# A new order of all operations up to the third set of the feed-forward, with ssm_k loaded in quarters ahead of v

## The chip, the core and the metric

The kernel runs on one core of a Trainium2 chip. Five engines work from queues of their own, each in the order of its queue: TensorE (PE, with its weight loads PEld), VectorE (DVE), ScalarE (ACT), GpSimd (POOL) and SyncE (SP), which issues all DMAs here. An instruction waits on semaphores of other engines, and everything behind it on its engine waits with it. The metric is the device time of one execution in microseconds. Before: 643.6 us, the median of 3 runs (643.42 to 643.73).

## The reference

```python
def _A_ref(q, k, v, shift_k, ssm_k, ssm_D):
    ...                                    # k_shift: causal depthwise conv of k, 4 taps
    kv = k_shift * v
    L = 2 * S
    ...                                    # y: irfft(rfft(kv) * rfft(ssm_k)) over S = 2048, per channel
    y = y + kv * ssm_D[None, None, :]
    return q * y
def _B_ref(x, w_gate, w_up, w_down):
    g = _silu(x @ w_gate)
    u = x @ w_up
    return (g * u) @ w_down
x = A_q
mod = (_silu(c) @ w_mod).reshape(c.shape[0], 6, 1, -1)
sa, ca, ga, sb, cb, gb = (mod[:, 0], mod[:, 1], mod[:, 2], mod[:, 3], mod[:, 4], mod[:, 5])
h = _layernorm(x, axis=-1) * (1 + ca) + sa
x = x + ga * _A_ref(h, A_k, A_v, A_shift_k, A_ssm_k, A_ssm_D)
h = _layernorm(x, axis=-1) * (1 + cb) + sb
x = x + gb * _B_ref(h, B_w_gate, B_w_up, B_w_down)
```

One sequence of 2048 tokens, 512 channels, 1792 hidden columns, all float32.

## The kernel before

**The convolution.** The 512 channels go in four blocks of 128 (index `c_` or `b`, 0 to 3). For a block, DVE (or ACT for the first tap) makes the four taps `u` from `kt` (`tap0`, `tap`), multiplies by `vt` (`times_v`), PE turns the product (`x_turn`, tile `kvt`, copied by ACT to `x`) and takes the first step of a transform (`x_first`, tile `s`, copied by ACT into `X`). The filter goes the same way: `k_first` (tile `s` from `ss`, the loaded ssm_k; ACT copies into `kt`) and `k_turn` (tile `kt`, copied into `K`). `load_e` loads the transform's matrix `er` in quarters, and `skip` adds ssm_D to one row of `ss` on DVE, which is why the quarter of `k_first` that holds this row waits for DVE.

**Sixteen pieces.** `X` and `K` of a block hold four pieces of 32 channels. For piece n, `swap_x` transposes 32 by 32 blocks of `X` in place (DVE), `x2nd` takes the second step (PE tile `px`, ACT copies it to `xs`), `product` takes it for `K` twice (PE tile `pk`) and multiplies with `xs` (two DVE operations `R`), and `inv` goes back (PE tile `iv`, ACT copies into the piece of `X`). A second `swap_x` by block follows on the blocks that are not stored; blocks 0, 1 and 2 are stored to memory instead (`put`, tile `away`) and read back in swapped order (`get`, `X<-away`), and block 3 is swapped by DVE. `y_pe` makes the outputs `y` of token set t (four sets of 512 tokens) and some blocks, `y_gate` multiplies them into `S1[t]` (tile `s`), and `add_c` or `add_y` adds that to `x`.

**The gate of layer norm.** `do_stats` (DVE, with four small operations on POOL that end in `rsa`), then `do_gate`: four ACT operations `s<-x,rsa` of 512 columns and two POOL operations `s<-s,bcs` of 2048 columns for one token set. `mod_load`, `mod_part`, `mod_bc`, `mod_T` and `mod_mix` make the six modulation vectors (tiles `wm`, `pb`, `part`, `pm`, `modT`, `bcs`).

**The feed-forward.** It takes 14 sets of 128 hidden columns for each half of the tokens. Sets 0 and 1 of the first half are written out one by one (`gu_pe`, `gu_act`, `gu_end`, tiles `g`, `sg`, `acts`), between the normalisations of token sets 0 and 1 (`norm2a`, `norm2b`: tile `n`; `norm_t`: tile `nt`; `norm_s`: tile `hraw`) and the splits into high and low parts (`op_hi`, `op_lo`, `w8_hi`, `w8_lo`, `wd_hi`, `wd_lo`). From the third set on (n = 2 to 27), `gate_up` computes two token sets with seven products (`seventh`, tiles `a`, `b`, `c`, `d`, six matmuls each) with four `down`s (tile `dn`, six matmuls each) between them; `split_w` prepares the next set's weights on ACT and POOL (`wa`, `sr`, `wsum`). The table `AT` hangs other work behind a product of a set; `half_t` is there the normalisation's turn for token sets 2 and 3 (two `nt` tiles, copied by ACT to `hraw`).

**What sets the order.** All engines are wrapped so that the program's order is kept: each engine executes its instructions in the order in which the code calls the helpers. Before, a loop over the 16 pieces (`loop`) with a table of hooks sets the order of the front: at each n `product(n)`, `x2nd(n + 1)`, `swap_x(n + 2)`, hooks, `inv(n - 1)`, hooks. The four PSUM buffers `ps` of two banks, the tags `e8` (8 buffers), `b16` (6), `r4` (5) and `f16` (1) are handed out as they come free.

In the profile nearly all instructions carry L40, the wrapper's line, so steps are told by their tiles.

Of the kernel before, what the change touches and what calls it, by code (L numbers as in the profile page):

```python
# [10 lines left out]
F32 = mybir.dt.float32  # L11
# [5 lines left out]
P = 128  # L17
# [26 lines left out]
def adaln_h3_swiglu(ctx, tc, q, kT, vT, shk, ssm, dskip, wgu, wdn, c, wmod, e_fwd, e_inv, w_c, out):  # L44
# [28 lines left out]
    def bank(name):  # L73
        return banks(name)[:, 0]
# [210 lines left out]
    def loop(hooks):  # L285
        for n in range(PIECES + 1):
            if n < PIECES:
                product(n)
            if n + 1 < PIECES:
                x2nd(n + 1)  # L290
            if n + 2 < PIECES:
                swap_x(n + 2)
            for f in hooks.get(n, ()):
                f()
            if n > 0:
                inv(n - 1)
            for f in hooks.get((n,), ()):
                f()

# [13 lines left out]
    def mod_part(i):  # L313

        ps = bank(f"pb{i}")
        for t in range(4):
            pe.matmul(ps[32 * t : 32 * t + 32], csb[:, t, :], WM[i][:, t, :], start=True, stop=True)
        part[i] = k2([P, D], F32, f"part{i}")
        act.copy(part[i], ps)
# [62 lines left out]
    def normal(dst, t, rs, both=True):  # L382

        for i in range(4):
# [9 lines left out]
    def gate(t):  # L394
# [328 lines left out]
    def load_ssm(c_):  # L723
        SS[c_] = e8([P, J, P], F32, f"ss{c_}")
        sp.dma_start(SS[c_], ssm[:, c_])
# [5 lines left out]
    load_k(0)  # L731
    load_e(0)
    load_e(1)
    load_ssm(0)
    load_e(2)
    load_e(3)
    load_v(0)
    load_k(1)
    load_v(1)
    wc = cp.tile([P, 4, 64], F32, name="wc")  # L740
    sp.dma_start(wc, w_c)
    W2, W2S, V1, V2 = (wc[:, i, :] for i in range(4))
    def kf(c_, *jqs):
        return [lambda jq=jq: k_first(c_, jq) for jq in jqs]

    def kt(c_, *ms):
        return [lambda m=m: k_turn(c_, m) for m in ms]

    def run(fs):
        for f in fs:  # L750
            f()

    tap0(0, dve)
    tap(0, 1)
    load_ssm(1)
    skip(0)
    run(kf(0, 0, 1, 2, 3))
    tap(0, 2)
    tap(0, 3)
    times_v(0, dve)  # L760
    x_turn(0, 0)
    x_turn(0, 1)
    x_first(0, 0)
    run(kt(0, 0, 1))
    x_first(0, 1)
    run(kt(0, 2, 3))
    tap0(1, dve)
    for t in range(1, KS):
        tap(1, t)
    load_k(2)  # L770
    swap_x(0)
    swap_x(1)
    x2nd(0)
    times_v(1, dve)
    load_v(2)
    tap0(2, act)
    skip(1)
# [5 lines left out]
    def do_stats(t):  # L783
        st1.append(stats(xt[t], f"a{t}"))

    def do_gate(t):
        if t < 2:
            S1[t] = e8([P, 4, D], F32, f"s{t}")
        else:
            if t == 2:  # L790
                S1["b"] = b16("s23", (P, 8, D))
            S1[t] = S1["b"][:, 4 * (t - 2) : 4 * (t - 1), :]
        gate(t)

    def add_c(t, *cs):
# [271 lines left out]
```

## Time and profile before

| what | value |
|---|---|
| median of 3 runs | 643.6 us |
| the profiled execution, its own time | 643.63 us |
| its span, first to last instruction | 641.9 us |
| PE busy | 601.9 us (94%) |
| DVE busy | 472.3 us (74%) |
| ACT, POOL busy | 299.5 us, 315.5 us |
| mean granted TensorE clock | 0.984 |
| first product of the third set (`a`) starts at | 232.29 us |

The profiled execution lies 1.73 us above its span, and at the median of the runs. Up to 232.29 us lies the front that the change reorders; behind it 26 sets of the feed-forward run at one speed. A busy share of PE is not a share of useful time where the granted clock is below 1.

### The profile page before, as it was taken

How to read it: one execution, taken by the hardware profiler on the slowest of the kernel's cores; microseconds unless marked ns; L12 is line 12 of the kernel's file. 1: busy time of each engine (PE TensorE's matmuls, PEld its weight loads, DVE VectorE, ACT ScalarE, POOL GpSimd, SP SyncE). 2: the span in 40 equal slices, each digit the busy share in tenths (PEclk: the TensorE clock that was granted, in tenths of full speed). 3: DMA queues.
4: the chain of work that ended last, by engine and by line, in shares of the span. 5: the costliest groups of instructions: out<-in, count | busy, mean ns of one | idle time of the engine just before them, and what ended most of it. 6: DMA issues, size and time to landing. Idle time of an engine off the chain costs nothing.

```text
span 641.9 us, 9081 instructions
## 1 busy us (share of the span) xinstructions
PE 601.9 (94%) x3604; PEld 454.8 (71%) x3604; DVE 472.3 (74%) x600; ACT 299.5 (47%) x439; POOL 315.5 (49%) x248
## 2 busy tenths in 40 slices
PE   2899999989697899999999999999999999999997
PEld 2756456534276788777778888878888888888885
DVE  5998767957978688877766886898565665656655
ACT  1867667874124545454544443544343333333320
POOL 0000000599254479775673767486565757575400
PEclk9999999989889999999999999999999999999999
DMA  8884492953931121302022111114210112120003
GB/s 293 370 300 161 165 234 86 269 103 137 242 115 66 34 67 33 99 33 67 20 79 66 34 34 65 34 66 154 75 67 34 65 38 86 43 65 1 0 2 131
DMA packets 30107, 64.68 MB, mean 101 GB/s; under 512 B 2289, under 2 KB 14705, under 8 KB 27506
## 3 DMA queue, kind: packets, MB, share of 16 engines
q1 hardware_dynamic: 30066, 64.11, 31.7%
q8 instruction: 28, 0.46, 0.3%
q14 instruction: 13, 0.11, 0.1%
HBM read 53.62 MB, written 10.49 MB: 100 GB/s over the span
## 4 chain that ended last, share of the span: by engine, by line
PE 54%; DVE 16%; ACT 5%; issue 2%; POOL 1%; ACTq 0%; DVEq 0%; POOLq 0%
PE dn L40 19%; PE b L40 9%; PE a L40 8%; PE c L40 8%; PE d L40 5%; DVE d L40 2%; DVE x L40 2%; PE y L40 2%; DVE acts L40 2%; DVE n L40 1%; DVE X L40 1%; ACT acts L40 1%; ACT op L40 1%; PE pk L40 1%; DVE c L40 1%
## 5 line engine op out<-in xcount | busy, mean ns | idle before, releaser
L40 PE MATMUL dn<-wd,acts 128*128 128x512 f32 x672 | 165.9, 390 | 0.5 <-DVE acts L40 0.5
L40 PEld LDWEIGHTS dn<-wd,acts 128*128 128x128 f32 x672 | 126.0, 188 | 27.9 <-DVE acts L40 1.1
L40 POOL TENSOR_TENSOR wa<-ws,wa 128x512 fp32r<-128x512 f32 (+1 forms) x52 | 60.6, 1188 | 110.9 <-ACT wa L40 103.1
L40 DVE TENSOR_TENSOR x<-x,dn 128x512 f32<-128x512 f32 x112 | 74.6, 680 | 54.4 <-PE dn L40 53.3
L40 PE MATMUL b<-op,wsum 128*128 128x512 f32 x312 | 79.7, 391 | 0.8 <-POOL wsum L40 0.8
L40 POOL TENSOR_TENSOR wsum<-sr,wsum 128x1024 fp32r<-128x1024 f32 x26 | 72.3, 2779 | 0.0
L40 PEld LDWEIGHTS b<-op,wsum 128*128 128x128 f32 x312 | 58.1, 188 | 13.3 <-POOL wsum L40 1.3
L40 POOL TENSOR_SCALAR rsa<-mva 128x4 f32<-128x4 f32 x8 | 2.5, 310 | 118.5 <-DVE mva L40 118.0
L40 PE MATMUL a<-op,wa 128*128 128x512 f32 x228 | 57.9, 389 | 0.0
L40 ACT ACTIVATE sg<-sg 128x512 f32<-128x512 f32 x26 | 16.5, 633 | 87.4 <-DVE sg L40 87.4
L40 DVE TENSOR_TENSOR R<-pk,xs 128x1024 f32<-128x1024 f32 x32 | 37.7, 1215 | 25.2 <-PE pk L40 25.2
L40 PEld LDWEIGHTS a<-op,wa 128*128 128x128 f32 x228 | 42.8, 188 | 8.9
L40 DVE STREAM_TRANSPOSE X<-X 128x1024 f32<-128x1024 f32 x20 | 45.3, 2277 | 0.1
L40 POOL TENSOR_TENSOR wd<-wds,wd 128x1024 fp32r<-128x1024 f32 x14 | 35.5, 2538 | 19.6 <-ACT wd L40 19.6
L40 ACT CAST acts<-d 128x512 fp32r<-128x512 f32 x26 | 15.3, 587 | 62.9 <-DVE d L40 36.5
L40 POOL TENSOR_TENSOR sr<-ws 128x256 f32<-128x256 f32 x52 | 43.1, 828 | 0.0
L40 PE MATMUL c<-op,wa 128*128 128x512 f32 x156 | 39.7, 390 | 0.0
L40 PE MATMUL d<-op,wsum 128*128 128x512 f32 x156 | 39.6, 389 | 0.0
L40 PE MATMUL c<-op,wsum 128*128 128x512 f32 x156 | 39.6, 389 | 0.0
L40 POOL TENSOR_TENSOR s<-s,bcs 128x2048 f32<-128x2048 f32 x8 | 36.5, 4568 | 0.3
L40 PE MATMUL pk<-K,wc 64*64 64x512 f32 x256 | 35.3, 626 | 1.1 <-ACT K L40 1.0
L40 DVE TENSOR_TENSOR op<-hraw,op 128x1024 fp32r<-128x1024 f32 x14 | 23.1, 1654 | 15.2 <-ACT op L40 15.2
(105 smaller groups left out, 1095.9 us busy)
## 6 DMA issues: line engine op xcount, KB each, us to landing
ws<-in_wgu SPq DMA_DIRECT2D x28, 512.0 KB, 3.3
wds<-in_wdn SPq DMA_DIRECT2D x14, 512.0 KB, 3.6
wm<-in_wmod SPq DMA_DIRECT2D x6, 1024.0 KB, 11.4
away<-X SPq DMA_DIRECT2D x3, 2048.0 KB, 7.5
X<-away SPq DMA_DIRECT2D x12, 512.0 KB, 11.2
kt<-in_kT SPq DMA_DIRECT2D x4, 1024.0 KB, 5.4
ss<-in_ssm SPq DMA_DIRECT2D x4, 1024.0 KB, 10.0
vt<-in_vT SPq DMA_DIRECT2D x4, 1024.0 KB, 10.1
```

What stands on the lines that cost most here:

```text
L40: return lambda *a, **k: self.tc.keep_in_program_order(f(*a, **k))
```

## The change

The hooks and the loop go. The calls from the first load to the end of set 1 now stand in one list of 324 calls, which sets the order on all engines; the operations are the same, with these differences: `load_ssm(0)` loads four quarters, two of them ahead of the matrix and all ahead of `v`; `times_v` is called by quarters, the stats and the four ACT operations of a gate by halves, the gate's POOL part by itself (`gate_p`); four `warm(6)` (six small matmuls that nothing reads) in place of one `warm(4)`; and `half_t` hangs one product later in its sets. `kx_first` and `swap_k` are new and called nowhere.

```diff
+    def gate_n(t, half):
+
+        if half == 0:
...
+        normal(lambda i: S1[t][:, i, :], t, st1[t], False, range(2 * half, 2 * half + 2))
+
+    def gate_p(t):
         s = S1[t]
-        normal(lambda i: s[:, i, :], t, st1[t], False)
         pool.tensor_tensor(s, s, bcs[:, None, 1, :].to_broadcast([P, 4, D]), op=ALU.mult)
         pool.tensor_tensor(s, s, bcs[:, None, 0, :].to_broadcast([P, 4, D]), op=ALU.add)
...
-    def load_ssm(c_):
-        SS[c_] = e8([P, J, P], F32, f"ss{c_}")
-        sp.dma_start(SS[c_], ssm[:, c_])
+    def load_ssm(c_, *jqs):
+        if c_ not in SS:
+            SS[c_] = e8([P, J, P], F32, f"ss{c_}")
+        for jq in jqs:
+            sp.dma_start(SS[c_][:, 4 * jq : 4 * jq + 4], ssm[:, c_, 4 * jq : 4 * jq + 4])
+        if not jqs:
+            sp.dma_start(SS[c_], ssm[:, c_])
...
+    warm(6)
+    warm(6)
+    load_k(0)
+    tap0(0, dve)
+    tap(0, 1)
+    load_ssm(0, 0)
+    load_ssm(0, 2)
+    load_e(2)
+    k_first(0, 2)
...
-        (5, 2): lambda: half_t(2, 0),
+        (5, 3): lambda: half_t(2, 0),
         (6, 7): lambda: norm2b(2, rs[2], 1),
-        (6, 2): lambda: half_t(2, 1),
-        (6, 3): lambda: norm_stats(3, range(0, 2)),
+        (6, 3): lambda: half_t(2, 1),
+        (6, 2): lambda: norm_stats(3, range(0, 2)),
...
-        (7, 2): lambda: half_t(3, 0),
+        (7, 3): lambda: half_t(3, 0),
         (8, 7): lambda: norm2b(3, rs[3], 1),
-        (8, 2): lambda: half_t(3, 1),
+        (8, 3): lambda: half_t(3, 1),
```

**The start, on SP.** The rows are the first large DMAs, before: `kt`, `vt` are k and v of a block, `ss` its filter, `er` the matrix in quarters.

```order
L40 DMA kt_93<-in_kT 128x2048
L40 DMA er<-in_e_fwd 128x512 x2
L40 DMA ss_97<-in_ssm 128x2048
L40 DMA er<-in_e_fwd 128x512 x2
L40 DMA vt_101<-in_vT 128x2048
L40 DMA kt_103<-in_kT 128x2048
L40 DMA vt_105<-in_vT 128x2048
L40 DMA wc<-in_w_c 128x256
L40 DMA ss_112<-in_ssm 128x2048
```

The same place in the changed kernel:

```order
L40 DMA kt_108<-in_kT 128x2048
L40 DMA ss_113<-in_ssm 128x512 x2
L40 DMA er<-in_e_fwd 128x512 x4
L40 DMA ss_113<-in_ssm 128x512 x2
L40 DMA vt_191<-in_vT 128x2048
L40 DMA wc<-in_w_c 128x256
L40 DMA kt_230<-in_kT 128x2048
L40 DMA ss_242<-in_ssm 128x2048
L40 DMA vt_293<-in_vT 128x2048
```

Two quarters of the first filter now stand ahead of the matrix, and the second block's filter ahead of its v.

**The gates, on ACT.** Before, around the gates of token sets 1, 2 and 3 (`s<-x,rsa`); `K_1255` is K of block 3, `X_642` X of block 2, `kt_1147` the filter of block 3 before its turn:

```order
L40 COPY xs<-px 128x1024
L40 ACTIVATE s_1140<-x_920,rsa_1058 128x512 x4
L40 COPY kt_1147<-s_1148 128x4x4x32 x2
L40 COPY kt_1147<-s_1159 128x4x4x32 x2
L40 COPY X_642<-iv 128x32x32
L40 COPY kt_1147<-s_1180 128x4x4x32 x2
L40 COPY kt_1147<-s_1191 128x4x4x32 x2
L40 COPY xs<-px 128x1024
L40 ACTIVATE s_1248<-x_922,rsa_1135 128x512 x4
L40 COPY K_1255<-kt 128x1024 x2
L40 COPY X_642<-iv 128x32x32
L40 COPY K_1255<-kt 128x1024 x2
```

In the changed kernel, around the gates of sets 1, 2 and 3 (`K_1221` is K of block 3, `X_747` X of block 2):

```order
L40 ACTIVATE s_1153<-x_834,rsa_1090 128x512 x4
L40 COPY X_747<-iv 128x32x32
L40 COPY xs<-px 128x1024 x2
L40 COPY X_747<-iv 128x32x32
L40 COPY K_1221<-kt 128x1024 x3
L40 COPY X_747<-iv 128x32x32 x2
L40 COPY K_1221<-kt 128x1024
L40 COPY xs<-px 128x1024
L40 ACTIVATE s_1306<-x_868,rsa_1166 128x512 x2
L40 ACTIVATE s_1306<-x_980,rsa_1322 128x512 x4
L40 ACTIVATE s_1306<-x_868,rsa_1166 128x512 x2
L40 COPY xs<-px 128x1024
```

The copies of K of block 3 moved ahead of the gates of token sets 2 and 3, which now stand together ahead of the copy to `xs` of piece 13.

**The last outputs, on PE.** Before, the end of the pieces and the first outputs of block 2 (`X_642`) and block 3 (`X_987`); `pb` are two modulation vectors:

```order
L40 MATMUL iv<-R,wc 64x512 x8
L40 MATMUL pk<-K_1255,wc 64x512 x8
L40 MATMUL iv<-R,wc 64x512 x16
L40 MATMUL y<-X_642,ei 64x128 x8
L40 MATMUL y<-X_987,ei 64x128 x8
L40 MATMUL pb_1535<-wm,csb 32x512 x4
L40 MATMUL pb_1542<-wm,csb 32x512 x4
```

In the changed kernel (`X_267` and `X_470` are X of blocks 0 and 1, `X_884` of block 3, `X_747` of block 2):

```order
L40 MATMUL iv<-R,wc 64x512 x16
L40 MATMUL y<-X_267,ei 64x128 x8
L40 MATMUL y<-X_470,ei 64x128 x8
L40 MATMUL pb_1545<-wm,csb 32x512 x4
L40 MATMUL y<-X_884,ei 64x128 x8
L40 MATMUL y<-X_747,ei 64x128 x8
L40 MATMUL warm<-ident 128x128 x6
L40 MATMUL pb_1587<-wm,csb 32x512 x4
```

An output of blocks 0 and 1 (token set 3) and one vector now stand between the last `iv` and the first output of block 3, and that one stands ahead of the one of block 2. On SP, `mod_load(3, 4)` moved from behind `get(2)` to ahead of it.

More of the change, by code (lines that the diff above doesn't have):

```diff
@@ L729, in skip, with load_wc @@
         dve.tensor_tensor(t, t, dsk[:, c_ * P : (c_ + 1) * P], op=ALU.add)
[L731 to L739, printed above, removed]
     wc = cp.tile([P, 4, 64], F32, name="wc")
-    sp.dma_start(wc, w_c)
     W2, W2S, V1, V2 = (wc[:, i, :] for i in range(4))
[L743 to L777, printed above, removed]
+    def load_wc():
+        sp.dma_start(wc, w_c)
     def mod_mix():
@@ new lines, in adaln_h3_swiglu @@
+    tap(0, 2)
+    tap(0, 3)
+    load_e(1)
+    load_ssm(0, 1)
+    k_first(0, 1)
+    load_ssm(0, 3)
+    k_first(0, 3)
+    k_turn(0, 0)
+    k_turn(0, 1)
+    load_v(0)
+    times_v(0, 3)
+    times_v(0, 2)
+    times_v(0, 1)
+    load_wc()
+    x_turn(0, 1)
+    k_turn(0, 3)
+    times_v(0, 0)
+    x_turn(0, 0)
+    load_k(1)
+    k_turn(0, 2)
+    load_ssm(1)
+    k_first(1, 2)
+    k_first(1, 1)
+    x_first(0, 0)
+    tap0(1, dve)
+    tap(1, 1)
+    tap(1, 2)
+    tap(1, 3)
+    load_v(1)
@@ new lines, in adaln_h3_swiglu @@
+    times_v(1, 3)
+    times_v(1, 0)
+    x_first(0, 1)
+    mod_load(1, 2)
+    mod_part(1)
+    k_first(1, 3)
+    skip(1)
+    times_v(1, 2)
+    times_v(1, 1)
+    k_first(1, 0)
+    mod_part(2)
+    x_turn(1, 1)
+    k_turn(1, 0)
+    load_k(2)
+    k_turn(1, 3)
+    swap_x(1)
+    swap_x(2)
+    tap0(2, act)
+    mod_bc(2)
+    x_turn(1, 0)
+    load_v(2)
+    swap_x(0)
+    k_turn(1, 1)
+    swap_x(3)
+    load_ssm(2)
+    skip(2)
+    k_turn(1, 2)
+    mod_bc(1)
+    tap(2, 1)
+    x2nd(0)
@@ new lines, in adaln_h3_swiglu @@
+    tap(2, 2)
+    tap(2, 3)
+    times_v(2, 2)
+    times_v(2, 3)
+    k_first(2, 3)
+    mod_load(0, 5)
+    times_v(2, 0)
+    x_first(1, 0)
+    x_first(1, 1)
+    mod_part(5)
+    k_first(2, 0)
+    load_ssm(3)
+    product(0)
+    x2nd(1)
+    x2nd(2)
+    swap_x(5)
+    load_k(3)
+    product(1)
+    tap0(3, act)
+    tap(3, 1)
+    skip(3)
+    times_v(2, 1)
+    k_first(2, 1)
+    inv(0)
+    k_first(2, 2)
+    inv(1)
+    tap(3, 2)
+    mod_part(0)
+    tap(3, 3)
+    k_turn(2, 0)
+    k_turn(2, 2)
@@ new lines, in adaln_h3_swiglu @@
+    k_turn(2, 1)
+    load_v(3)
+    product(2)
+    x2nd(3)
+    times_v(3, 0)
+    product(3)
+    x_turn(2, 0)
+    inv(2)
+    inv(3)
+    mod_bc(0)
+    times_v(3, 3)
+    x_turn(2, 1)
+    x_first(2, 0)
+    times_v(3, 1)
+    x_turn(3, 0)
+    times_v(3, 2)
+    load_x(0)
+    swap_x(4)
+    do_stats(0, 0)
+    k_turn(2, 3)
+    swap_x(6)
+    do_stats(0, 1)
+    x2nd(4)
+    product(4)
+    load_x(1)
+    x_turn(3, 1)
+    swap_x(7)
+    x_first(2, 1)
+    load_x(2)
+    swap_x(10)
+    swap_x(9)
@@ new lines, in adaln_h3_swiglu @@
+    k_first(3, 2)
+    x_first(3, 0)
+    do_stats(2, 0)
+    x2nd(5)
+    x_first(3, 1)
+    k_first(3, 3)
+    product(5)
+    swap_x(8)
+    x2nd(6)
+    swap_x(13)
+    x2nd(7)
+    load_x(3)
+    inv(4)
+    inv(5)
+    product(6)
+    put(0)
+    product(7)
+    mod_bc(5)
+    get(0)
+    mod_mix()
+    gate_n(0, 0)
+    inv(6)
+    inv(7)
+    put(1)
+    k_first(3, 1)
+    do_stats(1, 0)
+    do_stats(1, 1)
+    x2nd(8)
+    x2nd(9)
+    swap_x(11)
+    k_first(3, 0)
+    product(8)
+    product(9)
@@ new lines, in adaln_h3_swiglu @@
+    gate_n(0, 1)
+    gate_p(0)
+    gate_n(1, 0)
+    gate_n(1, 1)
+    gate_p(1)
+    do_stats(2, 1)
+    inv(8)
+    x2nd(10)
+    swap_x(14)
+    product(10)
+    x2nd(11)
+    swap_x(12)
+    inv(9)
+    k_turn(3, 0)
+    k_turn(3, 1)
+    k_turn(3, 3)
+    product(11)
+    load_einv()
+    swap_x(15)
+    inv(10)
+    inv(11)
+    k_turn(3, 2)
+    x2nd(12)
+    gate_n(2, 0)
+    do_stats(3, 0)
+    do_stats(3, 1)
+    gate_n(3, 0)
+    product(12)
+    gate_n(3, 1)
+    get(1)
+    gate_n(2, 1)
@@ new lines, in adaln_h3_swiglu @@
+    y_pe(0, 0, 1)
+    y_gate(0, 0, 1)
+    add_c(0, 0)
+    y_pe(1, 0, 1)
+    y_gate(1, 0, 1)
+    x2nd(13)
+    gate_p(3)
+    add_c(1, 0)
+    put(2)
+    inv(12)
+    x2nd(14)
+    product(13)
+    product(14)
+    swap_x(12)
+    inv(13)
+    mod_load(3, 4)
+    get(2)
+    swap_x(13)
+    warm(6)
+    x2nd(15)
+    product(15)
+    inv(14)
+    inv(15)
+    y_pe(3, 0, 1)
+    mod_part(3)
+    swap_x(14)
+    swap_x(15)
+    y_pe(0, 3)
+    gate_p(2)
+    add_c(0, 1)
+    y_pe(0, 2)
+    warm(6)
```

277 lines of the change are left out of this document (126 added, 151 removed).

## The prediction

> **What bounds the kernel now.** I read the timeline of PE first, to find where the feed-forward's steady run begins, then the busy times by stretch ahead of that point.
>
> ```profile
> 232.29 1.52 PE L40 MATMUL a<-op,wa 128*128 128x512 f32 x6
> ```
>
> This is the first product of the third set. Behind it PE runs nearly without a gap, and the only edit there is the place of `half_t`. So the question is when this row starts.
>
> ```profile
> core 0: us, PE busy (x) PEld busy (x) DVE busy (x) ACT busy (x) POOL busy (x), PEclk, DMA share, GB/s
> 0.00:12.31 12.31, 0.00 (x1) 0.01 (x1) 5.06 (x11) 1.49 (x2) 0.69 (x6) 1.00 0.74 249
> 12.31:42.00 29.69, 26.91 (x284) 21.43 (x288) 29.46 (x22) 21.47 (x25) 0.00 (x0) 1.00 0.84 334
> 42.00:112.00 70.00, 69.00 (x683) 37.34 (x676) 54.16 (x46) 48.28 (x60) 0.00 (x0) 1.00 0.61 182
> 136.00:152.00 16.00, 12.55 (x77) 4.41 (x75) 8.26 (x10) 10.75 (x14) 15.60 (x8) 0.79 0.01 5
> 152.00:182.00 30.00, 24.11 (x232) 11.75 (x234) 27.14 (x43) 7.51 (x10) 13.34 (x6) 0.83 0.96 264
> 182.00:204.00 22.00, 21.33 (x223) 18.90 (x220) 14.95 (x30) 8.72 (x11) 10.88 (x9) 1.00 0.13 48
> 204.00:216.00 12.00, 7.85 (x35) 6.16 (x33) 8.24 (x8) 8.36 (x11) 3.96 (x4) 0.86 0.15 46
> 216.00:232.29 16.29, 15.78 (x70) 13.06 (x70) 12.32 (x10) 6.11 (x9) 13.45 (x9) 1.00 0.11 33
> ```
>
> First number the length, then busy time by engine, granted clock, DMA. DVE fills 12 to 42 us (29.46 of 29.69), PE fills 42 to 112 (69.0 of 70). Behind 136 neither is full, and the clock falls below 1 in three stretches.
>
> **PE's work up to 232.29.** A step costs PE the distance to the next start where PE never waits:
>
> ```profile
> 45.61 1.95 PE L40 MATMUL pk<-K,wc 64*64 64x512 f32 x16
> 47.38 1.04 PE L40 MATMUL px<-X,wc 64*64 64x512 f32 x8
> 48.34 2.06 PE L40 MATMUL s<-er,ss 64*128 64x128 f32 x32
> 50.36 1.95 PE L40 MATMUL iv<-R,wc 64*64 64x512 f32 x16
> 52.23 2.06 PE L40 MATMUL s<-er,ss 64*128 64x128 f32 x32
> ...
> 100.24 2.06 PE L40 MATMUL kt<-ident,kt 128*128 128x128 f32 x16
> 102.14 1.88 PE L40 MATMUL pb<-part,sel 128*128 128x512 f32 x4
> 103.96 1.95 PE L40 MATMUL pk<-K,wc 64*64 64x512 f32 x16
> ...
> 152.23 1.97 PE L40 MATMUL y<-X,ei 128*64 128x128 f32 x32 [0.59 <-ACT X L40]
> 154.12 1.95 PE L40 MATMUL iv<-R,wc 64*64 64x512 f32 x16
> ...
> 233.65 1.52 PE L40 MATMUL b<-op,wsum 128*128 128x512 f32 x6
> 235.01 1.52 PE L40 MATMUL c<-op,wsum 128*128 128x512 f32 x6
> ```
>
> So `product` 1.77, `x2nd` 0.96, two `k_first` 2.02, `inv` 1.87, two turns about 2.0, a vector about 0.95, a `y` of two blocks 1.89, six large matmuls 1.36. Sixteen of each piece step: 28.3 + 15.4 + 30.0. `k_first` 16.5, `x_first` 15.9 (of the same shape), 24 turns 24.0, `y` 15.1, vectors 9.5 and their turns 1.9, `nt` 3.9, 96 `g` 21.8, 24 `dn` 5.4, `warm` 1.0: **188.8 us**. The row starts at 232.3, so PE loses **43.5 us** ahead of it.
>
> ```profile
> 7.67 1.28 DVE L40 TENSOR_SCALAR u<-kt,shk_sb 128x2048 f32<-128x2048 f32 x1 [3.16 <-DMA kt<-in_kT]
> 12.31 6.17 PE L40 MATMUL s<-er,ss 64*128 64x128 f32 x64 [12.31 <-DVE ss L40]
> 16.93 2.50 DVE L40 TENSOR_TENSOR vt<-u,vt 128x512 f32<-128x512 f32 x4
> 112.75 1.95 PE L40 MATMUL pk<-K,wc 64*64 64x512 f32 x16
> ...
> L40 DVE STREAM_TRANSPOSE X<-X 128x1024 f32<-128x1024 f32 x20 | 45.3, 2277 | 0.1
> L40 DVE SCALAR_TENSOR_TENSOR u<-kt,shk_sb,u 128x2047 f32<-128x2047 f32 (+2 forms) x12 | 28.0, 2329 | 0.3
> ```
>
> Where: 12.3 us ahead of the first matmul, 2.8 idle in 12 to 42, and 2.1 because the first 64 `s` take 6.17 us where the warm ones take 4.04: 17.2. The `pk` row at 112.75 is that of piece 9; ahead of it stand 94.5 us of the work above, so the loss is 18.2 by then: only 1 us more over 70, the running loss of a full PE, about 2%. The other 25 lie behind: 136 to 152 3.5 idle plus 0.21 of the clock, 6.8 together; 152 to 182 5.9 + 5.1 = 11.0; 204 to 216 4.2 + 1.7 = 5.8; little elsewhere.
>
> **The change: the start.** DVE has the path. It must do, ahead of the first `R`: two blocks with 1.28 + 3 x 2.33 + 2.50 each, 21.5; four swaps, 9.1; three taps and three quarters of `times_v` for block 2, 8.9; three skip adds, together about 0.8 by estimate: 40.3. From 7.67 that is 48.0. PE's list up to and with `product(0)` then ends at about 48.5, with 37.7 us of useful work done: a loss of **10.8** where it was 17.2. Loading the filter in quarters lets the first `k_first` run while DVE makes taps; that fills PE, not the path, and costs SP three more issues, hidden while data, not issues, fill the queue. If `v` came later by them, DVE would wait as long: k, filter, matrix and v are 4.19 MB, and v is wanted at 16.0.
>
> ```profile
> GB/s 293 370 300 161 165 234 86 269 103 137 242 115 66 34 67 33 99 33 67 20 79 66 34 34 65 34 66 154 75 67 34 65 38 86 43 65 1 0 2 131
> ```
>
> The first slice of 16 us moves 293 x 16.05 = 4.70 MB, so it is there. The two first `warm` stand in the wait and cost nothing.
>
> **The middle.** From `product(0)` to the outputs I added PE's and DVE's operations in the new order call by call: they stay within 3 us of each other, with steps of other pieces between each `product` and its `inv`. I take the same 2% of running loss, on 150 us: 3.0 (bounds 1 and 6). Splitting stats, gates and `times_v` changes no sum; the work that hides a split's later half is the other engine's queue.
>
> **The late part.**
>
> ```profile
> 134.64 9.17 POOL L40 TENSOR_TENSOR s<-s,bcs 128x2048 f32<-128x2048 f32 x2
> 134.72 2.93 ACT L40 ACTIVATE s<-x,rsa 128x512 f32<-128x512 f32 x4 [2.08 <-POOL rsa L40]
> 138.60 1.16 PE L40 MATMUL kt<-ident,kt 128*128 128x128 f32 x8 [2.13 <-ACT K L40]
> ...
> 152.20 0.34 SPq L40 DMA_DIRECT2D away<-X  x1
> 172.87 1.97 PE L40 MATMUL y<-X,ei 128*64 128x128 f32 x16 [3.93 <-DMA X<-away]
> ```
>
> (a) 136 to 152. Before, ACT waits for POOL's small `rsa` behind 9.2 us of gate work, and the copies of K that PE needs stand behind it. In the new order those copies stand ahead. What is late next is the copy to `xs` of piece 13, behind four pairs of ACT operations for sets 2 and 3 (twice the 2.93 of the row, 5.9 us) and behind `rsa` of set 2, which now has two gates ahead on POOL, 18.3 us. By my sum gate 0 starts near 114, `rsa` comes at 134, the copy at 141; PE has two `y`, two `x2nd` and an `inv` until then. I take 2 of the 6.8 (bounds 0 and 7).
>
> (b) 152 to 182. Block 2's way out and back took 172.87 - 152.20 = 20.7 us with the pieces nearly done. In the new order 28 us of PE work stand between `inv(11)` and the first `y` that reads it, so 3.9 us of wait and the slow clock behind it go; `wm` stands ahead of it on SP and takes some of the margin. Left is DVE: from `R` of piece 13 to the last swap three products at 2.4 and four swaps, 16.3 us, against 15.3 on PE, and a wait for the last two. I take 3.5 of 11.0 (bounds 2 and 8).
>
> (c) 204 to 216. Before, PE had only `n` of token set 1 to turn and waited for it; now products of sets 0 and 1 stand between. I take 2 of 5.8 (bounds 0 and 5).
>
> Sum of the loss: 10.8 + 3.0 + 2 + 3.5 + 2 = 21.3. PE's work: 188.8 - 1.0 + two `warm(6)` of about 1.4 = 190.6. The row comes at **211.9**, 20.4 earlier.
>
> The trace has the clock at 0.79 in 136 to 152 behind a gap of only 2.13 us in a stretch of thin work.
>
> [...]
>
> **The change: half_t.**
>
> ```profile
> 296.57 0.27 PE L40 MATMUL nt<-ident,n 128*128 128x128 f32 x1
> 298.05 0.98 PE L40 MATMUL nt<-ident,n 128*128 128x128 f32 x7 [1.22 <-DVE n L40]
> ...
> L40 PE MATMUL nt<-ident,n 128*128 128x128 f32 x32 | 5.0, 280 | 4.0 <-DVE n L40 4.0
> ```
>
> Four turns wait for `n`, 4.0 us together. One product later (1.36 us) the wait of 1.22 is covered; ACT's and DVE's orders do not change, and PE alone ends last there. I take **4.0** (bounds 3 and 4).
>
> **The sum.** 643.6 - 20.4 - 4.0 = **619.2**, from the profiled execution's 643.63 (span 641.9 and 1.7 around it), which is the runs' median. With all low bounds (loss 13.8) 612, with all high ones (36.8 less what cannot add, since a late `xs` also covers the swaps: about 28) 626.
>
> **Rivals.** *The wait moves to the first outputs.*
>
> ```profile
> 110.84 0.33 SPq L40 DMA_DIRECT2D away<-X  x1
> 119.26 7.11 SPq L40 DMA_DIRECT2D X<-away  x4
> 136.00:138.00 2.00, 0.47 (x5) 0.27 (x3) 1.61 (x5) 2.00 (x4) 2.00 (x1) 1.00 0.07 29
> ```
>
> Block 1 leaves at 110.84 and the queues are empty only from 136: 25 us, with the outputs' matrix among it. In the new order `y` of token set 0 stands ahead of four `inv`, with 27 us of PE work since block 1's last `inv`. The margin is 2 us. If it fails by 6, or if gate 0 starts as late as before and `rsa` comes 9 later, PE loses that and some 4 at the slow clock: **631** (626 to 638). For: the margin; against: block 2's trip took only 20.7.
>
> *Slower.* The clock. In 42 to 112 PE is full and the clock stays 1.00; at 136 to 138 PE is busy for 0.47 of 2 us, and slow matmuls follow. If the tight coupling of PE and DVE leaves PE short gaps everywhere, it runs slow from 20 to 200 us, and each 10 us at half clock costs 5 of progress. It outweighs the 24.4 from 50 slow microseconds on; at 70 it gives **654**. Against: the sums keep both engines full, and gaps of 1.2 us before cost no clock.
>
> [...]
>
> *The order brings nothing*, one engine's queue giving back elsewhere what it gains: 643.6.
>
> **Chances.** Forecast (612 to 626) 0.64; late outputs 0.20; better than 612 0.06; nothing 0.03; slower 0.07. The range 611 to 634 leaves out 0.05 below and some 0.15 above. About 0.2% can be told from no change: faster 0.90, same 0.03, slower 0.07.
>
> **What would show it.** `a` of the third set near 212. The first `R` near 48. `K` copies ahead of `s<-x,rsa`, and no PE gap of 2 us at the `kt` of block 3. No wait for `X<-away` at `y`. The wait of `nt` for `n` gone. It would be wrong if `y` of token set 0 waits for a DMA, if ACT waits for `rsa` past 140, or if the clock falls below 0.9 over more than 20 us.

## The result, and the profile after

The changed kernel took **620.37 us** (median of 4 runs, 619.95 to 620.67), the kernel before beside it 643.54 (643.42 to 643.73): a ratio of 0.9639, with a 95% interval of 0.9623 to 0.9656. Forecast were 619.2, in 611 to 634. The profiled execution is the run of 619.95, with a span of 618.2 us; its clock is 0.990 where it was 0.984.

The place that the prediction turned on, on PE's timeline of the changed kernel:

```profile
213.92 1.52 PE L40 MATMUL a<-op,wa 128*128 128x512 f32 x6
```

The third set starts 18.4 us earlier (232.29 before); forecast was 211.9, 20.4 earlier. Behind it the loop takes 618.2 - 213.92 = 404.3 us, where it took 641.9 - 232.29 = 409.6: 5.3 less, forecast 4.0. Together 23.7 of span. The busy times by stretch of the changed kernel, up to that row (length, then busy time by engine, the granted clock, the DMA share and GB/s):

```profile
0.00:8.60 8.60, 4.94 (x24) 4.75 (x24) 2.36 (x8) 1.49 (x2) 0.69 (x6) 1.00 0.66 215
8.60:48.00 39.40, 37.06 (x420) 31.66 (x420) 38.33 (x28) 32.68 (x45) 0.00 (x0) 0.91 0.99 385
48.00:112.00 64.00, 64.00 (x652) 33.85 (x654) 58.90 (x59) 45.74 (x57) 3.35 (x8) 1.00 0.58 177
112.00:136.00 24.00, 23.75 (x234) 12.25 (x228) 22.48 (x26) 16.84 (x20) 21.70 (x12) 1.00 0.98 227
136.00:152.00 16.00, 14.77 (x142) 6.11 (x142) 15.86 (x18) 8.05 (x10) 13.94 (x3) 1.00 1.12 248
152.00:182.00 30.00, 26.68 (x302) 19.74 (x295) 28.00 (x54) 11.59 (x14) 11.32 (x9) 1.00 0.36 101
182.00:212.00 30.00, 25.25 (x112) 20.77 (x111) 27.27 (x19) 13.94 (x21) 28.49 (x17) 0.94 0.16 53
```

Read the column of PE against the length: from 48 to 136 almost nothing is lost, and the clock is 1.00 to 182, also in 136 to 182, where it was 0.79 and 0.83. What is left stands at the two ends: the start, and the last 30 us, where POOL (28.49 of 30) and DVE (27.27) are nearly full and PE is not. That last stretch is the miss: 4.75 idle and 6% of clock on 30, 6.5 us, where 2 were forecast.

What PE waits for up to 214, longest group first, by the view of waits of the changed kernel (us in total, times, longest):

```profile
PE nt L40 <- DVE n L40: 4.4, 2, 3.0
PE s L40 <- DMA er<-in_e_fwd: 3.5, 1, 3.5
PE iv L40 <- DVE R L40: 1.8, 2, 1.2
PE dn L40 <- POOL wd L40: 1.7, 1, 1.7
```

No `y` waits for a block that comes back from memory. And in the chain of the changed kernel PE has 83% where it had 54%:

```profile
PE 83%; DVE 8%; ACT 3%; issue 2%; POOL 2%; DMA 1%; SPq 0%; ACTq 0%; DVEq 0%; POOLq 0%
```

### The profile page after: what moved, and what is told of

It reads as the page before. It is cut to its first block, busy times and chain, and to the rows that moved or that the text cites. A ratio compares the mean times of both kernels' runs of the same rounds, so it can differ in the third digit from the quotient of the medians.

```text
span 618.2 us, 9164 instructions
## 1 busy us (share of the span) xinstructions
PE 598.0 (97%) x3644; PEld 460.1 (74%) x3644; DVE 482.6 (78%) x601; ACT 298.7 (48%) x439; POOL 319.6 (52%) x248
## 4 chain that ended last, share of the span: by engine, by line
PE 83%; DVE 8%; ACT 3%; issue 2%; POOL 2%; DMA 1%; SPq 0%; ACTq 0%; DVEq 0%; POOLq 0%
PE dn L40 24%; PE a L40 11%; PE b L40 11%; PE c L40 11%; PE d L40 6%; PE s L40 5%; PE iv L40 3%; PE pk L40 3%; PE kt L40 3%; DVE R L40 2%; PE px L40 2%; DVE n L40 1%; PE pb L40 1%; PE kvt L40 1%; DVE x L40 1%
## 5 line engine op out<-in xcount | busy, mean ns | idle before, releaser
L40 POOL TENSOR_TENSOR wa<-ws,wa 128x512 fp32r<-128x512 f32 (+1 forms) x52 | 62.1, 1216 | 108.4 <-ACT wa L40 100.5
L40 PEld LDWEIGHTS b<-op,wsum 128*128 128x128 f32 x312 | 58.6, 188 | 12.2
L40 ACT ACTIVATE sg<-sg 128x512 f32<-128x512 f32 x26 | 16.5, 633 | 87.6 <-DVE sg L40 87.6
L40 DVE TENSOR_TENSOR acts<-c,acts 128x512 fp32r<-128x512 f32 x26 | 18.0, 691 | 21.8 <-ACT acts L40 21.8
L40 PEld LDWEIGHTS c<-op,wa 128*128 128x128 f32 x156 | 29.2, 188 | 6.3 <-DVE op L40 0.2
## 6 DMA issues: line engine op xcount, KB each, us to landing
wm<-in_wmod SPq DMA_DIRECT2D x6, 1024.0 KB, 12.4
```

The lines of the kernel that those rows point to most:

```text
L40: return lambda *a, **k: self.tc.keep_in_program_order(f(*a, **k))
```

## The experiments

Each kernel is the changed one with one edit, but for the sixth, which is the one before. All were timed in five rounds beside the kernel before. Two distances compare their traces better than absolute times: from the first `R` to the first `a` of the third set, and from there to the end of the span. The first `R` itself lies anywhere between 48.7 and 50.3 in the kernels whose start is that of the change.

| kernel | us, median | ratio to before, 95% | first `R` | `R` to `a` | `a` to end |
|---|---|---|---|---|---|
| as changed | 620.37 | 0.9623 to 0.9656 | 49.36 | 164.6 | 404.3 |
| 1 loads as before | 622.5 | 0.9660 to 0.9687 | 51.10 | 165.8 | 403.7 |
| 2 half_t back | 624.84 | 0.9705 to 0.9734 | 48.85 | 164.9 | 409.0 |
| 3 gates ahead of K | 632.77 | 0.9817 to 0.9852 | 49.45 | 176.3 | 404.3 |
| 4 no warm | 623.33 | 0.9669 to 0.9696 | 49.22 | 166.2 | 404.3 |
| 5 warm through | 622.34 | 0.9655 to 0.9697 | 48.40 | 168.2 | 403.9 |
| 7 n on ACT | 620.59 | 0.9632 to 0.9665 | 50.32 | 166.6 | 404.0 |
| 8 wd first | 621.63 | 0.9644 to 0.9670 | 50.18 | 164.9 | 405.3 |
| 9 adds late | 620.54 | 0.9625 to 0.9651 | 49.16 | 160.9 | 408.6 |
| 10 gate behind n | 622.75 | 0.9663 to 0.9689 | 49.60 | 167.0 | 404.3 |
| 11 warm late | 624.47 | 0.9685 to 0.9714 | 48.72 | 168.0 | 404.3 |
| 12 both of 7 and 8 | 619.96 | 0.9623 to 0.9649 | 48.93 | 164.9 | 404.0 |

**1. The loads of the start.**

```diff
+    load_e(0)
+    load_e(1)
+    load_ssm(0)
+    load_e(2)
+    load_e(3)
+    load_v(0)
...
-    load_ssm(0, 0)
-    load_ssm(0, 2)
-    load_e(2)
...
-    load_ssm(0, 3)
...
-    load_v(0)
```

> The changed kernel (620.4 us) with the loads of the start in the order of before: k, two quarters of the matrix, the first filter in one piece, the other two quarters, v. Theory: the new order of loads fills PE with the first k_first, but DVE has the path to the first R, so it is worth little: 620.5 to 622, first R within 1 us of 49.4. Rival: the loads bring the gain of the start (some 5 us): 624 to 627, first R at 53 or later.

It took 622.5, 2.1 more, with the first `R` at 51.10, 1.7 later: a little above the theory's range and well below the rival's. The timeline of DVE in this kernel shows by which way:

```profile
11.84 0.28 DVE L40 TENSOR_TENSOR ss<-ss,bcs 1x128 f32<-1x128 f32 x1 [1.08 <-DMA ss<-in_ssm]
31.98 2.31 DVE L40 STREAM_TRANSPOSE X<-X 128x1024 f32<-128x1024 f32 x1 [1.61 <-ACT X L40]
```

The skip add is one of DVE's operations and needs the filter, so with the whole filter in one transfer DVE itself waits 1.08; then its swaps wait 1.61 for X, which PE and ACT make, where they wait 0.56 in the changed kernel (at 30.26). The quarters are on DVE's path, not only on PE's. What the profiled execution loses beyond these 1.7 us is lost far behind the loads: from the first `dn` to `a` it takes 7.2 us where the changed kernel takes 5.6, partly at a clock of 0.50, behind a wait of 2.55 for `wd` (the last section has what the traces show of the clock behind a wait).

**5. More warm matmuls at the start.**

```diff
     warm(6)
     warm(6)
+    warm(6)
+    warm(6)
     load_k(0)
```

> The changed kernel with four warm(6) at the start in place of two, so that PE stays busy from 1.35 to about 9.5, when the first data come. Theory: the clock then stays at 1.00, but the first 64 s follow the arrival of the matrix and the filter, not the clock (without any warm they took 5.51 from 10.60 and ended at 16.1, where with two they took 6.70 from 9.77 and ended at 16.5), so the first R moves by less than 0.8 and the time is 619.6 to 620.6. Rival: the 2.7 us that slow matmuls cost the first s are on the path: 617.5 to 618.5.

PE's timeline, first of the changed kernel, then of this one:

```profile
1.35 4.94 PE L40 MATMUL warm<-ident 128*128 128x128 f32 x24 [1.35 <-POOL ident masks.py:199]
9.77 6.70 PE L40 MATMUL s<-er,ss 64*128 64x128 f32 x64 [3.48 <-DMA er<-in_e_fwd]
```

```profile
1.34 7.68 PE L40 MATMUL warm<-ident 128*128 128x128 f32 x48 [1.34 <-POOL ident masks.py:199]
9.78 1.16 PE L40 MATMUL s<-er,ss 64*128 64x128 f32 x16 [0.76 <-DMA er<-in_e_fwd]
11.44 3.27 PE L40 MATMUL s<-er,ss 64*128 64x128 f32 x48 [0.50 <-DMA er<-in_e_fwd]
```

The first `s` now run at full clock (1.00 in 8.6 to 48, where it was 0.91) and end at 14.7 rather than 16.5; the first `R` comes at 48.40, 0.96 earlier. So of PE's gain of 1.8 about half reaches `R`: between theory and rival, the two engines being that close. The time did not follow: 622.34, 2.0 more, with 168.2 from `R` to `a`. The loss is far behind the start, at the first `dn` on PE in this kernel:

```profile
206.86 2.77 PE L40 MATMUL dn<-wd,acts 128*128 128x512 f32 x6 [2.54 <-POOL wd L40]
211.02 5.74 PE L40 MATMUL dn<-wd,acts 128*128 128x512 f32 x18 [1.38 <-DVE sg L40]
```

This `dn` starts 1.5 us earlier than in the changed kernel (208.35), but PE has waited 2.54 for `wd` where it waits 1.71 there. The clock falls to 0.50 behind the wait, and from this `dn` to `a` it takes 9.7 us where the changed kernel takes 5.6. The interval touches that of the changed kernel, so I don't read a sign from it; the runs of this kernel spread from 621.69 to 625.04.

**4. No warm matmuls.** All four `warm(6)` are taken out.

```diff
-    warm(6)
-    warm(6)
...
-    warm(6)
...
-    warm(6)
```

> The changed kernel without the four warm(6), which nothing reads. Theory: the two at the start do nothing (the clock is at 0.50 from 10 to 16 us all the same), and PE waits less than 2.2 us in the places of the other two, so nothing or up to 1 us is lost: 619.5 to 621.5. Rival: the two later ones hold the clock in 136 to 182; without them it falls below 0.9 there: 623 to 627.

623.33, 3.0 more: the rival. The first `R` stands at 49.22, so the two at the start do nothing for it, as the theory had it. Without the other two, PE's wait at an `iv` grows from 0.66 to 2.27, and the clock falls. This kernel's row on PE's timeline, and its busy times in the stretches about and behind it:

```profile
153.80 3.48 PE L40 MATMUL iv<-R,wc 64*64 64x512 f32 x16 [2.27 <-DVE R L40]
```

```profile
152.00:156.00 4.00, 2.20 (x12) 0.67 (x16) 4.00 (x4) 0.61 (x1) 4.00 (x1) 0.76 1.14 248
156.00:160.00 4.00, 4.00 (x48) 2.00 (x40) 2.66 (x2) 1.01 (x1) 0.53 (x1) 0.81 0.57 217
```

In the second PE is busy for all 4 us, but at 0.81, behind the gap of 2.27. The profiled execution is the lowest of this kernel's four (621.47), so it shows only part of the 3.0.

**3. The gates of set 2 ahead of the copies of K.**

```diff
-    k_turn(3, 0)
-    k_turn(3, 1)
-    k_turn(3, 3)
     product(11)
...
     inv(10)
+    gate_n(2, 0)
+    gate_n(2, 1)
+    k_turn(3, 0)
+    k_turn(3, 1)
     inv(11)
+    k_turn(3, 3)
...
-    gate_n(2, 0)
...
-    gate_n(2, 1)
```

> The changed kernel with the gates of token set 2 put back ahead of the copies of K of block 3 on ACT, as before the change. Theory: the copies then wait behind POOL's rsa of set 2 (about 133) and PE has nothing for piece 12 until they are done: PE idle of 3 us or more between 125 and 145 and a clock below 1 there, 626 to 632. Rival: the order of these does not matter, the gap before the change had another cause (the time that block 3's pieces come at all): 620 to 622.

632.77: 12.4 more, the theory, a little beyond its range. The timeline of ACT, then of PE, in this kernel, and its busy times by stretch:

```profile
133.09 2.93 ACT L40 ACTIVATE s<-x,rsa 128x512 f32<-128x512 f32 x4 [7.28 <-POOL rsa L40]
135.92 1.90 ACT L40 COPY K<-kt 128x1024 f32<-128x1024 f32 x2
...
136.96 1.97 PE L40 MATMUL kt<-ident,kt 128*128 128x128 f32 x8 [7.28 <-ACT K L40]
```

```profile
112.00:136.00 24.00, 17.40 (x152) 7.14 (x144) 19.43 (x23) 11.31 (x15) 21.63 (x12) 0.97 0.74 143
136.00:152.00 16.00, 13.07 (x128) 7.30 (x128) 9.48 (x9) 11.33 (x14) 7.05 (x2) 0.84 0.81 279
```

ACT waits 7.28 us for POOL's `rsa`, and PE 7.28 for the K behind it. PE idles 24 - 17.40 = 6.6 in the first stretch and 2.9 in the second, and the clock of 0.84 costs 2.6 more: 12.1, where the changed kernel loses 1.5. In that one ACT makes the same gate at 133.06 with 0.62 of wait. The edit also moves three turns of K some steps back on PE, but the copies do not wait for these: the first two turns end at 126.71, and their copies start at 135.92, behind the gates. To undo this order alone costs half of the whole gain.

**2 and 6. half_t, undone and alone.** The second is the kernel before with the mirror image of this edit:

```diff
-        (5, 3): lambda: half_t(2, 0),
+        (5, 2): lambda: half_t(2, 0),
...
-        (6, 3): lambda: half_t(2, 1),
-        (6, 2): lambda: norm_stats(3, range(0, 2)),
+        (6, 2): lambda: half_t(2, 1),
+        (6, 3): lambda: norm_stats(3, range(0, 2)),
...
```

> The changed kernel with half_t at its old places in the last four sets' schedule. Theory: the four waits of nt for n come back, 4.0 us, nothing gives them back: 624.4 (623.5 to 625), and the nt row shows some 4 us of wait. Rival: the loop's later waits absorb it and the gain of the loop (409.6 to 404.3) has another source: 620.4 to 621.5.

> The kernel before with only the places of half_t (and of the norm_stats that changes places with it) taken from the change. Theory: the part is worth by itself what its undoing cost in the changed kernel (4.5 us, of which 4.0 are waits of nt): 639.0 to 639.8, and the wait of nt is gone. Rival: in the old order another wait takes its place: 641 or more.

Undone it costs 4.5 us (624.84), alone it brings 4.7 (639.13 beside 643.79; ratio 0.9931, 0.9918 to 0.9943): the part adds. PE's waits in the loop, of the kernel before with half_t moved, and then of the changed kernel with it moved back:

```profile
PE b L40 <- POOL wsum L40: 0.9, 1, 0.9
PE dn L40 <- DVE acts L40: 0.5, 2, 0.2
```

```profile
PE nt L40 <- DVE n L40: 4.0, 4, 1.2
```

The 4.0 of `nt` are there and gone as expected; 409.0 - 404.3 = 4.7 is the whole, 0.7 more than those four waits hold. The rest of the loop's 5.3 is the wait for `wsum`, 0.9, which the changed loop does not have, less 0.3 that its `dn` waits for ACT's `acts`; that the new order ahead of the loop takes the first away is argued, not shown.

**7, 8 and 12. What ends the last 30 us.** In the changed kernel, POOL and DVE behind the norm of set 1, and PE:

```profile
184.30 7.37 POOL L40 TENSOR_TENSOR x<-x,s 128x1024 f32<-128x1024 f32 x3
...
184.39 5.07 DVE L40 TENSOR_SCALAR n<-x,rsb 128x512 f32<-128x512 f32 x2 [0.59 <-POOL rsb L40]
...
189.51 3.15 PE L40 MATMUL nt<-ident,n 128*128 128x128 f32 x15 [3.04 <-DVE n L40]
...
208.35 5.74 PE L40 MATMUL dn<-wd,acts 128*128 128x512 f32 x24 [1.71 <-POOL wd L40]
```

Experiment 7 puts all four `n` on ACT, 8 moves `wd_lo(0)` on POOL, 12 does both:

```diff
-    norm2b(1, rs[1], 1)
-    norm2b(1, rs[1], 0)
+    norm2b(1, rs[1], 1, False)
+    norm2b(1, rs[1], 0, False)
...
+    wd_lo(0)
     split_w(2)
...
-    wd_lo(0)
     downs(1)
```

> The changed kernel with all four n of token set 1 on ACT, where before two stand on ACT and two on DVE. Theory: the two on DVE take 2.5 us each because POOL adds beside them, and PE's wait of 3.04 at nt (189.5) is theirs; on ACT four take some 3.1 us from 184.4, so nt comes at 187.5: 618 to 619. Rival: something else is late next (the hraw behind nt, or DVE's wds and op), and the time stays at 620 to 621.

> The changed kernel with POOL's wd_lo(0) ahead of its part of split_w(2). Theory: the wait of 1.71 of the first dn for wd (208.35) goes, and split_w ends 3.4 us later, at 208.3, which the third set's first a does not need before 211: 618.5 to 619.5. Rival: wsum of the third set is late in its place (b<-op,wsum waits), or the first dn then waits for acts: 620 to 621.5.

> The changed kernel with both edits that gained nothing alone: all four n of token set 1 on ACT, and wd_lo(0) ahead of split_w(2) on POOL. Theory: two chains end together ahead of the third set, DVE's n with what follows it and POOL's additions, split and wd; each edit alone only lets the other chain end last, and both together let PE run on: no wait over 1 us at nt or dn, first a of the third set 2 to 3 us earlier than with either alone (at 212.5 to 214, its start being some 1 later), 617.5 to 619. Rival: POOL's operations only move beside other work of DVE, which becomes as late as before (waits of PE for op, acts or sg): 620 to 622.5.

None gained. With 7 the wait of 3.04 for `n` is gone (0.38 is the longest left), and `dn` waits for `wd` 1.5 longer (its profiled execution, 622.73, is 2.1 above its median); with 8 `dn` no longer waits for `wd`, but six matmuls later for DVE's `sg`, and `R` to `a` stays at 164.9; what its profiled execution has more lies in the start and the loop (50.18 and 405.3). With both (619.96, the interval lies on that of the changed kernel) it is 164.9 once more. The three rows of `dn`, in this order:

```profile
208.58 8.53 PE L40 MATMUL dn<-wd,acts 128*128 128x512 f32 x24 [3.22 <-POOL wd L40]
```

```profile
210.83 4.37 PE L40 MATMUL dn<-wd,acts 128*128 128x512 f32 x18 [1.83 <-DVE sg L40]
```

```profile
208.02 6.00 PE L40 MATMUL dn<-wd,acts 128*128 128x512 f32 x18 [1.83 <-DVE sg L40]
```

So the rivals of all three hold, the times of 8 and 12 at most 0.13 outside their ranges.

**9 and 10. POOL's additions.** Experiment 9 puts the three additions of the first row above behind `wd_lo(0)`; 10 lets them start when `n` is done, by way of a gate on DVE that they wait for, and has `wd_lo(0)` first as 8 has.

```diff
-    add_y(3, 0, 4, (2, 3), pool)
...
-    add_y(3, 0, 4, (0, 1), pool)
...
-    add_y(2, 0, 4, (0, 1), pool)
...
     wd_lo(0)
+    add_y(3, 0, 4, (2, 3), pool)
+    add_y(3, 0, 4, (0, 1), pool)
+    add_y(2, 0, 4, (0, 1), pool)
```

and the tenth:

```diff
-    add_y(3, 0, 4, (2, 3), pool)
...
-    y_gate(2, 0, 1)
     norm2b(1, rs[1], 1)
     norm2b(1, rs[1], 0)
+    y_gate(2, 0, 1)
+    add_y(2, 0, 4, (0, 1), pool)
+    add_y(3, 0, 4, (2, 3), pool)
...
-    add_y(2, 0, 4, (0, 1), pool)
...
+    wd_lo(0)
     split_w(2)
...
-    wd_lo(0)
```

> The changed kernel with the three additions of y to x of sets 2 and 3 that stand on POOL at 184.3 put behind wd_lo(0); POOL then stands still from 184.4 until the split of the weights. Theory: the slow n on DVE (2.5 us each) come from POOL's additions beside them; alone they take the 1.33 of before, nt comes 2.3 us earlier, and the additions are needed by nobody before the norm of set 2: 618 to 619. Rival: the 2.5 us have another cause and the row of n stays at 5.07 for two: 620 to 621.

> The changed kernel with the gate of set 2's first output moved behind the two n of DVE, POOL's additions behind that gate (set 2's first), and wd_lo(0) ahead of split_w(2). POOL then starts adding when the n are done, and has finished before the loop. Theory: n takes 1.0 for two as with the additions late, dn no longer waits for wd, and the loop keeps its 404.3 since the additions are not in it: first a of the third set at 209 to 211, 616 to 617.5. Rival: the gain is given back once more (split_w later, b waits for wsum; or the bank of the output that is freed later holds up g): 619.5 to 621.

Experiment 9 shows the cause of the slow `n`, and where the gain goes. Its DVE, PE and ACT:

```profile
184.12 1.00 DVE L40 TENSOR_SCALAR n<-x,rsb 128x512 f32<-128x512 f32 x2 [0.58 <-POOL rsb L40]
...
214.71 1.43 PE L40 MATMUL c<-op,wsum 128*128 128x512 f32 x5 [1.56 <-DVE op L40]
...
216.95 1.05 ACT L40 CAST op<-hraw 128x1024 fp32r<-128x1024 f32 x1 [4.64 <-POOL x L40]
```

Two `n` take 1.00 us where they took 5.07, with nothing changed but that POOL stands still beside them. `R` to `a` falls to 160.9, 3.7 less. But ACT's `op` then waits 4.64 for the additions: by the code the outputs of sets 2 and 3 lie in one of six buffers of a size, of which `op` is the next to take one. The loop takes 408.6, 4.3 given back, and the time is 620.54, the same. Experiment 10 keeps the additions out of the loop, and they slow other work there. Its DVE:

```profile
184.61 1.00 DVE L40 TENSOR_SCALAR n<-x,rsb 128x512 f32<-128x512 f32 x2 [1.71 <-POOL rsb L40]
...
190.56 3.06 DVE L40 TENSOR_TENSOR op<-hraw,op 128x1024 fp32r<-128x1024 f32 x1 [0.28 <-ACT op L40]
193.55 3.43 DVE L40 TENSOR_TENSOR hraw<-hraw 128x1024 f32<-128x1024 f32 x1
196.90 2.88 DVE L40 TENSOR_TENSOR acts<-sg,acts 128x512 fp32r<-128x512 f32 x1
```

`n` is as fast, but `op` takes 3.06, `hraw` 3.43 and `acts` 2.88 us, where they took 1.23, 1.76 and 1.23 in the changed kernel; PE's `g` wait for `op` 1.65 and 2.14, and it took 622.75. The theory's first half held in both, its second in neither.

**11. Warm matmuls in the wait for n.**

```diff
+    warm(10)
     norm_t(1, 0)
     norm_t(1, 1)
```

> The changed kernel with one warm(10), some 2.7 us of matmuls that nothing reads, in the wait of PE for n of token set 1 (186.3 to 189.5). Theory: the clock of 0.73 and 0.84 in 188 to 196 comes of that wait; with PE busy it stays at 1.00, which is worth 4 x 0.27 + 4 x 0.16 = 1.7 us: 618.5 to 619.3. Rival: what PE does there is bound by DVE's n and the dn's wait for wd anyway, so a faster clock only lengthens that wait: 620 to 621.

624.47, 4.1 more, worse than both had it (the profiled execution, 622.81, is the third of its five). The clock does stay at 1.00 where it fell to 0.73, and the wait moves on to `dn`, as the rival said, with the slow clock behind it. Two stretches of this kernel, and a row of its PE:

```profile
188.00:192.00 4.00, 3.06 (x25) 2.76 (x24) 4.00 (x3) 1.35 (x2) 3.46 (x3) 1.00 0.00 0
...
208.00:212.00 4.00, 2.93 (x6) 1.83 (x6) 2.06 (x3) 0.00 (x0) 4.00 (x3) 0.57 0.36 131
```

```profile
208.20 2.93 PE L40 MATMUL dn<-wd,acts 128*128 128x512 f32 x6 [2.54 <-POOL wd L40]
```

## Why the prediction was right, point by point

The time was 1.2 us above the forecast; the steps behind it were less even. By the prediction's own terms, forecast and then measured from the stretches above:

| term | forecast | measured |
|---|---|---|
| loss at the start | 10.8 | 49.90 - 37.7 = 12.2 |
| running loss in the middle | 3.0 (1 to 6) | some 0.1, the rest of the sum |
| (a) 136 to 152 | 2 (0 to 7) | 16 - 14.77 = 1.2 |
| (b) 152 to 182 | 3.5 (2 to 8) | 30 - 26.68 = 3.3 |
| (c) the norm of set 1 | 2 (0 to 5) | 4.75 + 1.8 = 6.5 |
| all, ahead of `a` | 21.3 | 213.92 - 190.6 = 23.3 |
| the loop's gain | 4.0 (3 to 4) | 5.3, of which half_t 4.7 |

That the time came out so close is in part luck: ahead of `a`, (c) was set 4.5 too low and the start 1.4, the middle 2.9 too high and (a) 0.8, and the loop gained 1.3 more than forecast.

**The start** was right in its mechanism: DVE's list sets it, to within 1.4 us. Two of its rows in the changed kernel:

```profile
30.26 9.48 DVE L40 STREAM_TRANSPOSE X<-X 128x1024 f32<-128x1024 f32 x4 [0.56 <-ACT X L40]
...
49.36 2.36 DVE L40 TENSOR_TENSOR R<-pk,xs 128x1024 f32<-128x1024 f32 x2 [0.53 <-PE pk L40]
```

The step "that fills PE, not the path" failed. PE's and DVE's lists are within a microsecond of each other, the path changes over twice (swaps wait 0.56 for X, `R` 0.53 for `pk`), and the order of the loads is worth 1.7 us at the first `R`. That the two first `warm` cost nothing held (experiment 4); they also hold no clock, with 3.48 us of wait behind them: the first 64 `s` take 6.70 us there, longer than without them (5.51) and before (6.17), and 4.4 behind the four of experiment 5. The profile's clock of 1.00 at the start of before and of experiment 4 says nothing here: these traces hold no clock until 17.23 and 14.12 us, and a matmul of the first `s` of before lasts 417 ns in the median, as in the changed kernel at 0.50; at full clock it lasts 272 (experiment 5).

**(a)** was right, and experiment 3 shows the price: 12.4 us, more than the 6.8 that the old order lost there, since in the new one the gap opens ahead of 136 too. The gates stood where the sums put them: POOL's first at 112.60 (114 forecast), ACT's for set 2 at 133.06 (134), the copy to `xs` at 139.22 (141). The rival of the late outputs, which hung on these, did not come. ACT's gate of set 2 in the changed kernel:

```profile
133.06 1.52 ACT L40 ACTIVATE s<-x,rsa 128x512 f32<-128x512 f32 x2 [0.62 <-POOL rsa L40]
```

**(b)** was right in size. The step on `warm` in it failed: the prediction counted the two later ones as 2.8 us of work and gave them no use. They are worth their cost and 3.0 us more (experiment 4), of which the clock of 0.76 and 0.81 without them shows a part. That block 2's return is covered is read from the trace, where no `y` waits for it; no experiment moved it.

**(c)** is the term that was mis-sized: "now products of sets 0 and 1 stand between. I take 2 of 5.8 (bounds 0 and 5)"; it is 6.5, above the upper bound. That step counted PE's products, and not what DVE and POOL do beside each other. Three additions, two `n`, a split and `wd` meet there, and several operations of DVE beside one of POOL took twice to over five times their time (`wds` 2.79 us where it took 1.22 in experiment 9, `n` 5.07 for two where they took 1.00 there). Experiment 9, where the additions are away from it, takes 3.7 less from `R` to `a`, which is most of the 4.5. The middle, which lost nothing where 3.0 were set, hid most of the miss.

**half_t** was right in its mechanism, 0.7 low in its size. The rival that the clock goes slow from 20 to 200 us was wrong: it is 1.00 in all stretches from 48 to 182 of the profiled execution.

What stays open is whether (c) can be had for less. Five orders of it (7, 8, 10, 11, 12) gave between 619.96 and 624.47, and none is surely faster than the change; 9 gained 3.7 there and lost 4.3 behind it. A copy of the two sets' buffer that frees `op` earlier was not tried. Experiments 5 and 11, whose edits lie apart, both end with 168 us from `R` to `a`, and their rows of `dn` agree on why. In both PE waits 2.54 for `wd`, the clock falls to 0.50 behind it, and the first six `dn` take 2.77 and 2.93 us (1.52 in experiment 8). DVE's operations behind these come late in their turn, so the other `dn` wait 1.38 for `sg` in both.

## What to carry to other kernels

Where an engine has to wait for a slow neighbour, let it do first whatever it already can: to put the copies of K back behind a gate that waits for POOL cost 12.4 us, half of what this change brought. Count a DVE operation beside a busy POOL at the length of POOL's operation too, not at its own alone: in experiment 10 `op` took 3.06 us beside additions of 3.02, where it took 1.23 in the changed kernel; `sg`, which reads PE's output from PSUM, kept its 0.68 beside additions. Before 2 or 3 us between two kernels are put down to an edit, look whether a wait somewhere else has cost one of them its clock: in experiment 5 it stood at 0.50 behind 2.54 us of wait, and from the first `dn` to `a` it took 9.7 us, 5.6 in the changed kernel. And when a stretch is bound by two engines together, as the one of experiments 7 and 8, an edit that moves one operation may only move the wait; look at what comes free late before moving work out of it (experiment 9 gained 3.7 us and gave 4.3 back).

## What the runs showed of the hardware

Several of DVE's operations took longer beside POOL's, by very different factors: one `n` of 128x512 takes 0.50 us with POOL standing still (experiment 9) and 2.5 beside an addition of POOL, and an addition on DVE, elsewhere 0.67, takes 3.74 in the changed kernel beside POOL's gate operations (137.98 to 156.73):

```profile
139.37 3.74 DVE L40 TENSOR_TENSOR x<-x,s 128x512 f32<-128x512 f32 x1
...
189.37 0.68 DVE L40 TENSOR_TENSOR sg<-sg,g 128x512 f32<-128x512 f32 x1
```

The second row stands beside POOL's additions too (184.30 to 191.67) and takes no longer than elsewhere (0.67 and 0.68 at 197.53 and 210.64); its `g` is PE's output in PSUM. The two slow `n` last 5.07 us, and two of POOL's three additions 2 x 7.37 / 3 = 4.9. In experiment 10 the three take 9.07, 3.02 each, and `op`, `hraw` and `acts` beside them and `wd` 2.88 to 3.43: an operation of DVE there takes about as long as one of POOL. By what the one engine holds up the other, no run here shows.

The granted clock in these traces is 1.00 or 0.50 (0.73 over 4 us is a mixture), and by its records in all 14 traces it changes only at multiples of 3.41 us from its first change. In them a slow stretch went with how full PE had been in such a window, not with the length of a gap by itself. The wait for `n` of token set 1 is 3.04 us in the changed kernel and in experiment 1. These are two windows about it, first of the changed kernel, then of experiment 1:

```profile
186.46:189.87 3.41, 0.37 (x4) 0.36 (x4) 3.41 (x3) 0.53 (x1) 3.41 (x3) 1.00 0.00 0
189.88:193.29 3.41, 3.41 (x16) 3.24 (x15) 2.88 (x2) 2.27 (x3) 2.28 (x2) 0.50 0.00 0
```

```profile
186.64:190.05 3.41, 1.51 (x8) 0.96 (x6) 3.41 (x2) 1.53 (x3) 3.41 (x2) 1.00 0.00 0
190.05:193.46 3.41, 2.27 (x18) 2.19 (x19) 3.41 (x3) 1.25 (x2) 3.41 (x3) 1.00 0.00 0
```

In the first the wait fills one window, with PE busy for 0.37 us of it, and the next runs at 0.50. In the second the border of two windows splits the wait, PE is busy for 1.51 and 2.27, and the clock stays at 1.00. Counted over the 14 traces, from the first change to 8 us ahead of the end: all 27 windows at full clock in which PE was busy for less than 0.44 of the time were followed by a slow one, none with more than 0.61 was, and in between 7 of 24 were. The wait for `n` at the first `nt` that has one (about 172) is 1.35 us in experiment 5 and in the changed kernel: in experiment 5 PE was busy for 2.05 us of the window's 3.40, and a slow one followed; in the changed kernel for 2.50 of 3.41 (169.40 to 172.81), and none did. The gap of 2.27 us in experiment 4 leaves PE busy for 1.14 us of 3.41 (150.66 to 154.07), and a slow one followed.

The windows lie elsewhere in each execution: the first change comes between 4.20 and 7.04 us in the kernels that start with warm matmuls. So one execution can lose clock at a wait that costs another none, as at the 3.04 us above; that this makes the spread of experiment 5 (621.69 to 625.04) is not shown. The first data come at 9.77 us in one run and at 11.00 in another with the same start (experiment 8); the first `R` follows, 49.36 and 50.18, so a single trace's start is known to about a microsecond.
